# Gate and up products written to PSUM in unit order, with the stride moved into VectorE's transpose

## Chip, cores, metric

The kernel runs on one core of one Trainium2 chip. The metric is device time in microseconds (us) of one execution; a profile of one execution goes with each kernel. PE is TensorE, PEld the weight load that comes before each of its matmuls, DVE is VectorE, ACT is ScalarE. "Granted clock" is the share of full TensorE speed that the trace records.

## The reference, cut to what matters

One decode step of a transformer layer for one token: layer norm, attention over a cache of 4096 positions for 32 heads, a residual add, then layer norm and a gated MLP, which is where the change lies.

```python
# ... attention: q = norm(x) @ wq; softmax(q k^T) v for 32 heads x 4096 keys x 128; @ wo ...
g = jnp.einsum("bsd,df->bsf", x, w_gate)    # x: 1 x 640, w_gate: 640 x 1728
u = jnp.einsum("bsd,df->bsf", x, w_up)
h = _gelu(g) * u
return jnp.einsum("bsf,fd->bsd", h, w_down)  # w_down: 1728 x 640
```

All inputs are bf16. Four fifths of the 84.23 MB read are the K and V caches, each 32 x 4096 x 128 x 2 bytes = 33.6 MB.

## The kernel before

The MLP has one row of activations. Four row groups of the PE array (r = 0..3, output rows 0, 32, 64, 96) each compute 432 of the 1728 units, so that four matmuls run side by side; five such rounds (j, the chunks of 128 of the 640 inputs) accumulate. The 432 units of a row are 16 groups `i` of 27; each group serves two partitions `b`, 14 units `c` each (one unit is shared), hence 448 output columns. A transpose of 32x32 blocks on VectorE then turns each row into columns, so that unit values lie on partitions for the w_down product.

```python
DF = 1728; PER = 2; PAIR_UNITS = 27; NFC = 14; HP = 32; COLS = NFC * HP   # 448; values filled in here
WD = ((0, 8), (8, 11), (11, 13), (13, 14))     # w_down is loaded in four pieces of chunks

def up(ps, w, name):
    landed_once(name)                          # PE waits for the weights
    for j in range(DC):                        # 5
        for r in range(YR):                    # 4
            rhs = ...                          # [128, 16, 2 (step 13), 14]: runs of 14 bf16
            inst = PE.matmul(
                ps[32 * r : 32 * r + 1, :].rearrange("q (c i b) -> q i b c", c=NFC, b=PER),
                lhsT=hc[:, j : j + 1], rhs=rhs, start=False, stop=(j == DC - 1),
                skip_group_check=True, tile_position=(0, 32 * r))
    return inst

PE.wait_ge(S["dve"], D_HC)
end("g", up(g_ps, wg_sb, "wg"))
fill(6)                                        # fillers: matmuls nobody reads, meant to hold the PE clock up
end("u", up(u_ps, wu_sb, "wu"))
fill(2)
PE.wait_ge(S["dve"], D_HID)
for i, (a, b) in enumerate(WD):
    PE.wait_ge(S[f"wd{i}"], 16 * PER)          # y's matmuls wait for each piece of w_down
    for c in range(a, b):
        ...                                    # 4 matmuls of 160 columns each
end("y", inst)
# [cut] VectorE:
def turn_rows(col, ps):
    dve(lambda: DVE.transpose(col[:].rearrange("p c n -> p (c n)"), ps), False)

wait_pe(T["end", "g"]); turn_rows(g_col, g_ps)
# [cut] ten small operations of the GELU
wait_pe(T["end", "u"]); turn_rows(u_col, u_ps)
# [cut] hid_own, hid = gelu(g) * u;  then y_row = y_ps + h_row, and the store
# [cut] sync engine, in this order, one queue:
load("wg", ...); load("wu", ...)
SP.wait_ge(S["dve"], D_SCORES[NQ - SLOTS])
for i, (a, b) in enumerate(WD):
    for odd in range(PER):
        load(f"wd{i}", ...)                    # eight transfers, the last of the program's inputs
```

In the old order, consecutive outputs of a matmul (c, the innermost of its loop) lie 32 fp32, that is 128 bytes, apart in PSUM; the transpose reads its row contiguously.

The softmax here doesn't subtract the row's maximum and nothing guards it: scores larger than these inputs give would overflow.

Of the kernel before, what the change touches and what calls it, by code (L numbers as in the profile page):

```python
# [9 lines left out]
def kernel(  # L10
# [19 lines left out]
    PE, DVE, ACT, SP, POOL = nc.tensor, nc.vector, nc.scalar, nc.sync, nc.gpsimd  # L30
# [20 lines left out]
    PER = 2  # L51
    PAIR_UNITS = PER * DF // P
    NFC = (PAIR_UNITS + 1) // 2
# [102 lines left out]
    def tick(which, inst):  # L156
        inst.then_inc(S[which], 1)
        done[which] += 1
        return done[which]
# [6 lines left out]
    def wait(engine, which, value):  # L166
        if value > 0:
            engine.wait_ge(S[which], value)
# [8 lines left out]
    def landed_once(name):  # L177

        PE.wait_ge(S[name], 16)
        once.append(name)  # L180
# [4 lines left out]
    def dve(make, raw=True):  # L185

        if raw:
            wait(DVE, "dve", done["dve"])
        return tick("dve", make())
# [199 lines left out]
    def up(ps, w, name):  # L389


        landed_once(name)
        for j in range(DC):
            for r in range(YR):
                rhs = w[:, j, r * RG : (r + 1) * RG].rearrange("p (i f) -> p i f", f=PAIR_UNITS)
                rhs = bass.AP(
                    tensor=rhs.tensor,
                    offset=rhs.offset,
                    ap=[rhs.ap[0], rhs.ap[1], [PAIR_UNITS - NFC, PER], [1, NFC]],
                )  # L400
                inst = PE.matmul(
                    ps[32 * r : 32 * r + 1, :].rearrange("q (c i b) -> q i b c", c=NFC, b=PER),
                    lhsT=hc[:, j : j + 1],
                    rhs=rhs,
                    start=False,
                    stop=(j == DC - 1),
                    skip_group_check=True,
                    tile_position=(0, 32 * r),
# [5 lines that stand above are left out]
    fill(6)  # L414
# [3 lines that stand above are left out]
# [179 lines left out]
            turn_keys(m + 1, 1)  # L597

    def turn_rows(col, ps):
        dve(lambda: DVE.transpose(col[:].rearrange("p c n -> p (c n)"), ps), False)  # L600

    assert done["dve"] == D0
    wait_pe(pe_at(NQ - 1, "project"))
# [5 lines left out]
    assert var_of(hm, hv) == D_HV  # L609
    wait_pe(T["end", "g"])  # L610
    turn_rows(g_col, g_ps)
    DVE.wait_ge(S["r"], 2)
    dve(lambda: DVE.tensor_scalar(g_sb[:], g_col[:, :, 0], hr[:], None, op0=ALU.mult))
# [10 lines left out]
    dve(lambda: DVE.tensor_tensor(g_own[:], g_sb[:, ends], parity[:], op=ALU.mult))  # L624
    wait_pe(T["end", "u"])
    turn_rows(u_col, u_ps)
    dve(lambda: DVE.tensor_tensor(hid_own[:], g_own[:], u_col[:, ends, 0], op=ALU.mult))
    assert dve(lambda: DVE.tensor_tensor(hid[:], g_sb[:], u_col[:, :, 0], op=ALU.mult), False) == D_HID
# [50 lines left out]
```

## Time and profile before

| | before |
|---|---|
| time, median of three runs | 205.8 us (205.79 to 205.98) |
| bytes read from HBM | 84.23 MB, 413 GB/s over the span |
| busy: PE / DVE | 45% / 52% of the span |
| gate products (20 matmuls) | 190.27 to 194.17 us, clock 0.50 |
| up products (20 matmuls) | 195.78 to 197.83 us, clock 1.00 |
| the two row transposes | 0.65 us each |
| hid ready | 198.81 us |
| last y matmul ends | 200.91 us |

From the page of the kernel before: the span, two engines, and two rows that cut the span into 40 slices (tenths of DMA busy time, and GB/s moved).

```profile
span 203.9 us, 4088 instructions
...
PE 90.8 (45%) x1839; PEld 53.8 (26%) x1839; DVE 105.2 (52%) x185; ACT 4.5 (2%) x11; POOL 6.8 (3%) x12
...
DMA  7999999999999999999989999999899999999990
GB/s 249 410 466 411 418 456 437 437 411 416 450 434 386 463 450 424 418 424 444 444 381 467 450 418 418 431 437 456 383 424 437 431 418 437 431 418 433 421 375 23
```

The DMA engines are full from the second slice nearly to the end, so the kernel is as long as its bytes plus what comes before the first and after the last of them. PE and VectorE are each about half idle. A change to either matters only if its work lies after the last bytes, or holds up a transfer.

The chain of waits, the last pieces in order of time (start us, length us, what):

```profile
176.91 23.69 DMA big<-in_B_w_down_dram
...
200.64 0.27 PE y L378 x4
...
200.94 0.32 DVE y_row L630
```

One w_down transfer, queued at 176.91 us behind everything else, lands at 200.60, and only four y matmuls and an add follow it. Gate and up are not in the chain. The tail in the timeline (start us, length us, engine, line, what, [idle time before, and what ended it]):

```profile
190.27 3.90 PE L401 MATMUL g<-big,hc 128*1 128x448 bf16 x20
...
194.11 1.74 PE L369 MATMUL s<-ex,ident 128*128 128x512 bf16 x6
194.23 0.65 DVE L600 STREAM_TRANSPOSE g_col<-g 128x448 f32<-128x448 f32 x1 [3.44 <-PE g L401]
...
195.78 2.05 PE L401 MATMUL u<-big,hc 128*1 128x448 bf16 x20
...
197.88 0.65 DVE L600 STREAM_TRANSPOSE u_col<-u 128x448 f32<-128x448 f32 x1 [0.42 <-PE u L401]
...
198.64 0.17 DVE L628 TENSOR_TENSOR hid<-g_sb,u_col 128x14 bf16<-128x14 f32 x1
...
198.88 0.99 PE L378 MATMUL y<-big,hid 128*1 128x160 bf16 x42
...
200.28 0.60 PE L378 MATMUL y<-big,hid 128*1 128x160 bf16 x10 [0.41 <-DMA big<-in_B_w_down_dram]
200.64 0.08 PEld L378 LDWEIGHTS y<-big,hid 128*1 128x1 bf16 x2 [0.26 <-DMA big<-in_B_w_down_dram]
...
200.94 0.32 DVE L630 TENSOR_TENSOR y_row<-y,h_row 128x160 bf16<-128x160 f32 x1 [2.12 <-PE y L378]
```

Compute is ahead: 44 y matmuls run at once after hid, and then PE stands until 200.28 us for the third piece of w_down, and its weight loads until 200.64 us for the fourth and last. Five rounds of four gate matmuls took 3.9 us at half clock, and the same five rounds of up 2.05 us at full clock.

### The profile page before, as it was taken

The numbers are of one execution on the slowest core, as the hardware profiler recorded it, in microseconds if no ns is written. First come the engines' busy times: TensorE is split into PE (matmuls) and PEld (weight loads), VectorE is DVE, ScalarE is ACT, GpSimd is POOL, SyncE is SP. The second block draws the span as 40 slices with busy tenths as digits, with TensorE's granted clock in tenths as the row PEclk, the third lists the DMA queues.
The fourth block names the chain that finished last, engine by engine and source line by source line (L and its number), as shares of the span: only waits on it lengthen the run. The fifth ranks groups of instructions, "written<-read, shape, count | busy, mean of one in ns | idle before, by whom it ended". The sixth has DMA issues, their size and how long they took to land. (4 is left out here: it accounts for less than half of the span.)

```text
span 203.9 us, 4088 instructions
## 1 busy us (share of the span) xinstructions
PE 90.8 (45%) x1839; PEld 53.8 (26%) x1839; DVE 105.2 (52%) x185; ACT 4.5 (2%) x11; POOL 6.8 (3%) x12
## 2 busy tenths in 40 slices
PE   0003603516642862066307640484166358258993
PEld 0001100115312711062107310451063154046221
DVE  5003399480649467509570957064908582632260
ACT  2000100000000000000000000000000000000000
POOL 8301000000000000000000000000000000000100
PEclk9999965555555555556755555555555755555597
DMA  7999999999999999999989999999899999999990
GB/s 249 410 466 411 418 456 437 437 411 416 450 434 386 463 450 424 418 424 444 444 381 467 450 418 418 431 437 456 383 424 437 431 418 437 431 418 433 421 375 23
DMA packets 4405, 84.30 MB, mean 413 GB/s; under 512 B 560, under 2 KB 688, under 8 KB 944
## 3 DMA queue, kind: packets, MB, share of 16 engines
q1 hardware_dynamic: 4400, 84.23, 96.8%
q8 instruction: 3, 0.05, 0.1%
q14 instruction: 2, 0.02, 0.0%
HBM read 84.23 MB, written 0.00 MB: 413 GB/s over the span
## 5 line engine op out<-in xcount | busy, mean ns | idle before, releaser
L561 DVE STREAM_TRANSPOSE big<-big 128x1024 f32<-128x1024 f32 x64 | 73.7, 1210 | 6.4 <-issue 4.0
L273 PE MATMUL o<-ex,big 128*128 128x4 bf16 x1024 | 28.6, 166 | 37.0 <-PEq L173 37.0
L245 PE MATMUL s<-big,q_quad 128*8 128x512 bf16 x256 | 28.7, 594 | 23.8 <-DVE big L561 23.8
L273 PEld LDWEIGHTS o<-ex,big 128*128 128x128 bf16 x1024 | 28.4, 104 | 37.4 <-issue 37.4
L588 DVE TENSOR_TENSOR o_col<-o,rinv 128x4 bf16<-128x4 f32 x8 | 1.3, 162 | 37.2 <-PE o L273 37.2
L245 PEld LDWEIGHTS s<-big,q_quad 128*8 128x8 bf16 x256 | 7.0, 112 | 40.7 <-DVE big L561 32.1
L570 DVE STREAM_TRANSPOSE s_turned<-s 128x512 f32<-128x512 f32 x8 | 5.7, 717 | 14.3 <-PE s L245 14.3
L280 PE MATMUL a<-wo,o_row 128*1 128x160 bf16 x256 | 9.9, 333 | 2.3 <-DVE o_row L595 2.3
L292 PE MATMUL t<-rs_cur,ones_f 128*128 128x4 f32 x16 | 4.7, 366 | 10.1 <-DVE rs_cur L581 10.1
L573 DVE TENSOR_TENSOR ex<-e,of_head 128x512 bf16<-128x512 f32 x8 | 5.5, 691 | 6.8 <-PE e L261 6.8
L302 PE MATMUL o<-x_col,mean_f 128*128 128x10 f32 x2 | 0.6, 376 | 16.7 <-DVE x_col L210 16.7
L280 PEld LDWEIGHTS a<-wo,o_row 128*1 128x1 bf16 x256 | 7.1, 115 | 3.0 <-DVE o_row L595 3.0
L261 PE MATMUL e<-e_part,ident 128*32 128x32 bf16 x128 | 2.5, 196 | 10.1 <-PEq L340 10.1
L292 PEld LDWEIGHTS t<-rs_cur,ones_f 128*128 128x128 f32 x16 | 4.0, 313 | 11.1 <-DVE rs_cur L581 11.1
L445 POOL TENSOR_TENSOR hr<-hv,half_f 128x1 f32<-128x1 f32 x1 | 0.6, 553 | 172.1 <-DVE hv L219 172.1
L223 DVE CAST x_row<-x_69 128x160 f32<-128x160 bf16 x1 | 0.2, 243 | 11.5 <-DMA x_69<-in_A_x_dram 11.5
L261 PEld LDWEIGHTS e<-e_part,ident 128*32 128x32 bf16 x128 | 1.8, 106 | 16.4 <-issue 16.4
L513 ACT ACTIVATE e_part<-s_turned 128x128 bf16<-128x128 f32 x8 | 2.5, 308 | 153.2 <-DVE s_turned L570 153.2
L302 PEld LDWEIGHTS o<-x_col,mean_f 128*128 128x128 f32 x2 | 0.5, 313 | 16.7 <-DVE x_col L210 16.7
L295 PE MATMUL o<-col_of,o_spread 128*128 128x8 bf16 x8 | 1.5, 188 | 7.0 <-issue 3.5
L441 POOL MEMSET wo<- 128x5120 bf16 x1 | 4.4, 4368 | 0.0
L318 PE MATMUL g<-big,xn_bf 128*1 128x512 bf16 x20 | 3.2, 623 | 1.9 <-DVE xn_bf L230 1.9
(84 smaller groups left out, 48.1 us busy)
## 6 DMA issues: line engine op xcount, KB each, us to landing
big<-in_A_k_cache_dram SPq DMA_DIRECT2D x7, 4096.0 KB, 20.2
big<-in_A_v_cache_dram SPq DMA_DIRECT2D x6, 4096.0 KB, 17.7
big<-in_A_v_cache_dram SPq DMA_DIRECT2D x4, 2048.0 KB, 12.3
big<-in_A_wq_dram SPq DMA_DIRECT2D x1, 5120.0 KB, 15.2
wo<-in_A_wo_dram SPq DMA_DIRECT2D x4, 1280.0 KB, 15.6
big<-in_A_k_cache_dram SPq DMA_DIRECT2D x2, 2048.0 KB, 17.2
big<-in_B_w_gate_dram SPq DMA_DIRECT2D x1, 2160.0 KB, 18.5
big<-in_B_w_up_dram SPq DMA_DIRECT2D x1, 2160.0 KB, 23.2
```

What stands on the lines that cost most here:

```text
L245: inst = PE.matmul(s_bank[32 * r : 32 * r + 2 * QH, :], lhsT=q_quad[:, 2 * k + e, (1 - b) * QH : (3 - b) * QH], rhs=kt_at[:, k, HALF * b + ...
L261: inst = PE.matmul(to[32 * h : 32 * h + 32, r], lhsT=ident[:, 32 * r : 32 * r + 32], rhs=e_part[:, :, :, h], start=True, stop=True, tile_p ...
L273: inst = PE.matmul(o_ps, lhsT=vt[:, j, :], rhs=e_t[:, j, :], start=(j == 0), stop=(j == NB - 1))
L280: inst = PE.matmul(attn_ps[32 * r : 32 * r + 1, :], lhsT=o_row[:, j : j + 1], rhs=wo_t[:, j, r * YW : (r + 1) * YW], start=False, stop=j = ...
L292: mark("totals", PE.matmul(ps, lhsT=ones_f[:], rhs=rs_cur[:], start=True, stop=True))
L295: inst = PE.matmul(ps, lhsT=o_spread[:].rearrange("p h c -> p (h c)"), rhs=col_of[:], start=True, stop=True)
L318: inst = PE.matmul(qr_ps[b][32 * r : 32 * r + 1, :], lhsT=xn_bf[:, c : c + 1], rhs=wq_sb[:, c, :].rearrange("p (m h d) -> p m h d", h=QH, ...
L441: POOL.memset(t[:], 0.0).then_inc(S["pool"], 1)
L513: ACT.activation(e_part[:].rearrange("p b j h -> p j b h"), s_turned[:, :, 0 : 2 * QH].rearrange("p j (b h) -> p j b h", b=2), AF.Exp, sca ...
L561: DVE.transpose(to[:, c], of[:, c].rearrange("p (j k n) -> p j k n", k=2, n=HP)).then_inc(S["kt"], 1)
L570: assert dve(lambda: DVE.transpose(s_turned[:].rearrange("p j n -> p (j n)"), s_bank[:]), False) == D_SCORES[m]
L573: DVE.tensor_tensor(e_t[:], e_ps.unsqueeze(2).broadcast_to(shape), of_head[:].unsqueeze(1).broadcast_to(shape), op=ALU.mult,).then_inc(S[" ...
```

## The change

The output is written in the order i, b, c, so that a matmul writes 448 consecutive fp32; VectorE's transpose picks up every 14th fp32 instead. Nothing else differs, and the order of instructions on every engine is the same. The intent is to speed up the products.

```diff
@@ up() @@
-                    ps[32 * r : 32 * r + 1, :].rearrange("q (c i b) -> q i b c", c=NFC, b=PER),
+                    ps[32 * r : 32 * r + 1, :].rearrange("q (i b c) -> q i b c", c=NFC, b=PER),
@@ turn_rows() @@
-        dve(lambda: DVE.transpose(col[:].rearrange("p c n -> p (c n)"), ps), False)
+        dve(lambda: DVE.transpose(col[:], ps.rearrange("q (p c) -> q c p", c=NFC)), False)
```

## The prediction

> **What bounds the kernel now.** The memory queue. The page's slices show the 16 DMA engines 90% or more busy in nearly every slice of the 203.9 us span (84.23 MB at 413 GB/s); PE is busy 45%, VectorE 52%. The chain of waits ends in one 23.69 us piece, the last w_down transfer (176.91 to 200.60 us), then 0.27 us of y matmuls, 0.32 us of the last add, and the store.
>
> **The stage that changes.** From the timeline of the tail: 20 gate matmuls 190.27 to 194.17 us at granted clock 0.50; six fillers to 195.85; 20 up matmuls 195.78 to 197.83 at clock 1.00; the two row transposes 0.65 us each; hid ready at 198.81; 44 y matmuls 198.87 to 199.86; then PE waits twice for w_down (until 200.28 and 200.64). Without those waits y would end near 200.15, not 200.91 (estimate: 199.86 plus twelve matmuls at the same pace). So compute is already about 0.8 us ahead of the last bytes.
>
> **What the change does.** No instruction is added, removed or moved on any engine. Two access patterns change.
> 1. Gate and up matmuls write 448 consecutive fp32 of PSUM instead of 128-byte steps. Now four concurrent row groups of 448 columns take 0.74 us at clock 0.50 and 0.38 us at 1.00, about twice per column what the query matmuls pay (512 columns, contiguous, about 0.445 us a group at 0.5). The Trainium skill, "PSUM — Partial Sum Buffer", Specifications, says any non-contiguous pattern slows matmuls significantly; this trace agrees, by a factor of about 2. I expect gate near 2.0 us (3.9 before) and up near 1.0 us (2.05).
> 2. The two transposes read PSUM in 56-byte steps. The trace's contiguous ones (448 elements 649 ns, 512 elements 717 ns) extrapolate to about 343 ns for 160; the strided 160-element one takes 461 ns. Scaled to 448 this estimates 0.98 us each, +0.33; range 0.8 to 1.3.
>
> Gate values come about 1.6 us earlier, but up waits for the fillers and its weights (issued about 172.0, 23.2 us to landing, so about 195.2); it starts about 0.5 us earlier, ends about 1.5 us earlier, and hid comes about 1.2 us earlier (near 197.6).
>
> **How much is critical.** None. The last w_down bytes still land near 200.6; the gain becomes a longer PE wait for w_down. No DMA issue depends on these instructions: the queue's last wait for compute before the store (near 171 us) lies before the changed stage.
>
> **Second order.** PE idles more from 197 to 200 us, so its clock could fall to 0.5 before the last y matmuls: at most +0.1 to 0.2 us.
>
> **Prediction:** 205.8 us, range 205.3 to 206.2; faster by over 2%: 0.01, within 2%: 0.98, slower: 0.01.
>
> **What would show it right.** Gate matmuls spanning about 2.0 us, up about 1.0; the g and u transposes near 980 ns; hid about a microsecond earlier; y's waits on w_down longer in sum; the chain still ending in w_down near 200.6 us; total within 0.3 us.
>
> **What would make it wrong.** If the doubled matmul time comes from the moving operand (runs of 14 elements), not the output, gate and up stay slow, and the dearer transposes delay hid by 0.3 to 0.7 us: still inside the slack, still about 205.8. If a strided transpose cost over 1.5 us, hid would pass the last bytes and the time would rise by tenths. If the last bytes land earlier than read here, a gain could show, at most about 0.7 us, well under 2%.

## The result, and the profile after

| | before | after |
|---|---|---|
| time, median of four runs each | 205.86 us (205.79 to 205.98) | 205.90 us (205.80 to 206.03) |
| gate products, from first start to last end | 3.90 us | 2.04 us |
| up products | 2.05 us | 1.18 us |
| one row transpose | 649 ns | 650 ns |
| hid ready | 198.81 us | 197.80 us |
| end of PE's last wait for w_down | 200.64 us | 200.94 us |

The ratio is 1.0002, 95% interval 0.9985 to 1.0019: no change is seen, and one of more than 0.2% is excluded. A ratio here is always the mean time of one kernel's fast runs over that of the other kernel's fast runs of the same rounds, so it is not quite the ratio of the medians quoted. Results are correct. The two profiles are of single executions at the two ends of the spread: the one before took 205.66 us, less than any of the timed runs above, and the one after 206.03 us, the slowest of its four.

The same rows of the page, after:

```profile
span 204.2 us, 4088 instructions
...
PE 89.1 (44%) x1839; PEld 53.7 (26%) x1839; DVE 105.2 (52%) x185; ACT 4.5 (2%) x11; POOL 6.8 (3%) x12
...
DMA  7999999999999999999999999999999999999980
GB/s 249 401 474 411 411 456 456 424 411 416 443 452 391 456 443 417 411 449 443 436 386 481 424 411 424 456 443 424 394 428 433 430 420 433 430 423 432 416 359 19
```

The same bytes at the same pace; PE lost 1.7 us of busy time. The chain of waits, last pieces:

```profile
175.68 24.86 DMA big<-in_B_w_down_dram
200.58 0.70 PE y L378 x12
201.30 0.33 DVE y_row L630
```

It still runs through a w_down transfer. The one that it names lands at 175.68 + 24.86 = 200.54 us, but it is the third piece, and the chain before named the fourth. The chain view misses the wait for the fourth here, since by the modelled ends some of the matmuls from 200.58 us were still running when it landed. The timeline shows it: the weight loads of the last four matmuls waited until 200.94 us. The tail:

```profile
190.31 2.04 PE L401 MATMUL g<-big,hc 128*1 128x448 bf16 x20
...
192.28 1.99 PE L369 MATMUL s<-ex,ident 128*128 128x512 bf16 x6
192.40 0.65 DVE L600 STREAM_TRANSPOSE g_col<-g 128x448 f32<-128x448 f32 x1 [1.57 <-PE g L401]
...
195.63 1.18 PE L401 MATMUL u<-big,hc 128*1 128x448 bf16 x20 [1.36 <-DMA big<-in_B_w_up_dram]
...
196.87 0.65 DVE L600 STREAM_TRANSPOSE u_col<-u 128x448 f32<-128x448 f32 x1 [1.23 <-PE u L401]
...
197.63 0.17 DVE L628 TENSOR_TENSOR hid<-g_sb,u_col 128x14 bf16<-128x14 f32 x1
...
198.78 0.23 PE L378 MATMUL y<-big,hid_own 128*1 128x160 bf16 x2 [1.43 <-DMA big<-in_B_w_down_dram]
...
198.78 0.72 PE L378 MATMUL y<-big,hid 128*1 128x160 bf16 x30
...
199.82 0.38 PE L378 MATMUL y<-big,hid 128*1 128x160 bf16 x12 [0.32 <-DMA big<-in_B_w_down_dram]
...
200.58 0.66 PE L378 MATMUL y<-big,hid 128*1 128x160 bf16 x10 [0.38 <-DMA big<-in_B_w_down_dram]
200.94 0.08 PEld L378 LDWEIGHTS y<-big,hid 128*1 128x1 bf16 x2 [0.26 <-DMA big<-in_B_w_down_dram]
...
201.30 0.33 DVE L630 TENSOR_TENSOR y_row<-y,h_row 128x160 bf16<-128x160 f32 x1 [3.49 <-PE y L378]
```

Compare line by line. The gate products are 1.86 us shorter. Up starts only 0.15 us earlier, since it now waits 1.36 us for its weights; it is 0.87 us shorter, and hid comes 1.01 us earlier. Then PE waits for all four pieces of w_down (until 198.78, 199.82, 200.58 and 200.94 us). The saved microsecond has become waiting time there.

The last add starts at 201.30 us instead of 200.94, 0.36 us later. Of this 0.30 us is the landing: PE's last wait ended at 200.94 us and not at 200.64. The landing records say the same (200.90 against 200.60 us; they are semaphore updates kept in the packed trace, of which `prof` prints only the waits that they end). They also show a spread: with w_down in eight transfers the last piece landed at 200.60, 200.76 and 200.89 us in three traces of the kernel before and its variants, and at 200.73 to 201.05 us in six of the changed kernel and its variants. The two ranges overlap; whether the change has any part in the shift is not shown, and the times of the two kernels do not differ. The other 0.06 us goes with the granted clock, which the windows view shows (columns: stretch, its length, busy time of each engine with the number of instructions, PE clock, DMA share, GB/s):

```profile
199.80:200.90 1.10, 0.62 (x18) 0.19 (x12) 0.00 (x0) 0.00 (x0) 0.00 (x0) 1.00 0.09 27
```

```profile
200.50:201.30 0.80, 0.67 (x12) 0.19 (x12) 0.00 (x1) 0.00 (x0) 0.00 (x0) 0.50 0.00 0
```

In this run of the changed kernel the clock had fallen to 0.50 for the last y matmuls. The 0.70 us of the last twelve in the chain is not the price of that, since it holds the wait until 200.94 us. Experiment 4 comes back to it.

### The profile page after: what moved, and what is told of

Its sections match the earlier page's. It is cut to its first block, busy times and chain, and to the rows that moved or that the text cites. A ratio compares the mean times of both kernels' runs of the same rounds, so it can differ in the third digit from the quotient of the medians.

```text
span 204.2 us, 4088 instructions
## 1 busy us (share of the span) xinstructions
PE 89.1 (44%) x1839; PEld 53.7 (26%) x1839; DVE 105.2 (52%) x185; ACT 4.5 (2%) x11; POOL 6.8 (3%) x12
## 5 line engine op out<-in xcount | busy, mean ns | idle before, releaser
L245 PE MATMUL s<-big,q_quad 128*8 128x512 bf16 x256 | 29.6, 609 | 24.1 <-DVE big L561 24.1
L223 DVE CAST x_row<-x_69 128x160 f32<-128x160 bf16 x1 | 0.2, 244 | 11.4 <-DMA x_69<-in_A_x_dram 11.4
L369 PE MATMUL s<-ex,ident 128*128 128x512 bf16 x11 | 4.2, 499 | 0.0
## 6 DMA issues: line engine op xcount, KB each, us to landing
big<-in_B_w_up_dram SPq DMA_DIRECT2D x1, 2160.0 KB, 23.5
```

The lines of the kernel that those rows point to most:

```text
L245: inst = PE.matmul(s_bank[32 * r : 32 * r + 2 * QH, :], lhsT=q_quad[:, 2 * k + e, (1 - b) * QH : (3 - b) * QH], rhs=kt_at[:, k, HALF * b + ...
L369: PE.matmul(s_bank[:], lhsT=ident[:], rhs=e_t[:].rearrange("p j h -> p (j h)"), start=True, stop=True)
```

## The experiments

My theory: the change does what was meant in its stage, about 1.0 us, and the w_down transfer covers all of it. Its rivals: the stage does not really get shorter to its end (up waits for its weights, so nothing but idle time is won); or the end is set by something else than w_down; or something gained is given back elsewhere (transposes, clock).

### 1. Take the w_down transfers away, from both kernels

```diff
-    SP.wait_ge(S["dve"], D_SCORES[NQ - SLOTS])
-            load(f"wd{i}", ...)
+            pass
-        PE.wait_ge(S[f"wd{i}"], 16 * PER)
-        POOL.sem_inc(S[f"wd{i}"], -16 * PER)
```

The y products then read old K data: the result is wrong.

> The kernel before without its w_down transfers (y then reads old K data: wrong on purpose). My theory: w_down's landing is what ends both kernels, and compute stands only 0.8 us behind it here, so the time falls by 0.6 to 1.0 us, to about 205.0 us, and the chain of waits ends in y, hid and the up transpose instead of a w_down transfer. Rival (the end is set by compute, or by something fixed): no change, or the fall is that of 2.2 MB at 413 GB/s, about 5 us.

> The changed kernel without its w_down transfers (wrong on purpose). My theory: with the transfer gone the saving of the change becomes visible: hid was ready 1.0 us earlier (197.80 against 198.81), so this is 0.8 to 1.4 us faster than before_nowd, about 204.0 us. Rival (the change saves nothing of the tail because up waits for its weights, whatever the matmuls take): within 0.3 us of before_nowd.

Measured in the same rounds: kernel before 205.97 us; before without w_down 204.67 us (ratio 0.9947, 0.9932 to 0.9961); after without w_down 203.66 us (ratio 0.9890, 0.9875 to 0.9905). The two differ by 1.01 us (medians of five and of four runs; 0.85 us between the two profiled runs), as the theory said, and the intervals do not overlap. The timeline of each without w_down:

```profile
195.49 2.05 PE L401 MATMUL u<-big,hc 128*1 128x448 bf16 x20
...
198.59 1.13 PE L378 MATMUL y<-big,hid 128*1 128x160 bf16 x52
```

```profile
195.42 1.26 PE L401 MATMUL u<-big,hc 128*1 128x448 bf16 x20 [0.29 <-DMA big<-in_B_w_up_dram]
...
197.73 1.13 PE L378 MATMUL y<-big,hid 128*1 128x160 bf16 x52
```

No y matmul waits any more, and y starts right after hid. The fall of 1.30 us of the kernel before is more than the 0.6 to 1.0 us that I expected. Part of this is that I reckoned from the profile before, whose run was 0.31 us faster than the median here (205.66 against 205.97 us). Part is seen in the profile: up started at 195.49 us there and not at 195.78, as the six fillers ahead of it took 1.47 us and not 1.74 (the clock had risen earlier). y ended at 199.75 us instead of 200.91, 1.16 us sooner; less those 0.29 us, the slack in front of w_down is 0.87 us. The rival of 5 us (the bytes themselves) is out, because the tail's compute, not the transfer, then ends the kernel.

### 2. Make the tail's compute longer by the same amount, in both kernels

```diff
     end("u", up(u_ps, wu_sb, "wu"))
-    fill(2)
+    fill(18)
```

> The kernel before with 16 more filler matmuls (about 3.45 us at full clock) between the up matmuls and y, w_down loaded as usual. My theory: the fillers eat the 0.8 us of slack and the rest shows: y starts near 201.65, ends near 202.95 instead of 200.91: +1.7 to +2.3 us, about 207.9 us. Rival (slack is larger than I read): less than +1 us.

> The changed kernel with the same 16 fillers. My theory: up ends 1.0 us earlier, so y starts near 200.65 and ends near 201.95: +0.6 to +1.2 us, about 206.9 us, which is 0.8 to 1.2 us less than before_fill. Rival (the change has no effect on when hid or up end): same as before_fill within 0.3 us.

Measured: before with the fillers 207.47 us (ratio 1.0087, 1.0073 to 1.0101), after with the fillers 206.52 us (ratio 1.0030, 1.0016 to 1.0043), against 205.97 us for the kernel before. The timeline of y in each, in that order:

```profile
201.49 1.12 PE L378 MATMUL y<-big,hid 128*1 128x160 bf16 x52
```

```profile
200.75 1.13 PE L378 MATMUL y<-big,hid 128*1 128x160 bf16 x52
```

Both rises (1.50 and 0.55 us) are a little under what I expected, because I had again reckoned from the fast run of the profile before: between single profiles they are 1.74 us (207.40 - 205.66) and 1.01 us (206.67 - 205.66), inside both expectations. The difference of the medians, 0.95 us, is what the theory gives; between the two profiled runs it is 0.73 us, as up waited for its weights until 195.64 us in the second and started at 195.51 us in the first. With w_down loaded as always, the microsecond appears in the time once compute is the later of the two. So the change does shorten the stage to its end, and the rival that only idle time is won falls.

### 3. What a step costs, measured by itself

Into the idle start of the changed kernel, before x and wq arrive, went eight transposes on VectorE and, after 16 warming matmuls, six sets of twelve matmuls (three rounds of the four row groups, 448 columns each). The operand is the matrix that streams through the array (`rhs`); an "even" one is read without gaps, the kernel's own comes in runs of 14.

```diff
+    dve(lambda: DVE.transpose(flat, src))                                      # SBUF, 448, contiguous
+    dve(lambda: DVE.transpose(g_col[:], src.rearrange("q (p c) -> q c p", c=14)))  # SBUF, step 14
+    ...                                        # the same for 160 (step 5), and all four from PSUM (g_ps)
+    PE.matmul(...)  # L355 even operand, contiguous output
+    PE.matmul(...)  # L358 operand in runs of 14, contiguous output    (the changed kernel)
+    PE.matmul(...)  # L361 operand in runs of 14, output "q (c i b)"   (the kernel before)
+    PE.matmul(...)  # L364 even operand, output steps of 128 bytes
+    PE.matmul(...)  # L367 even operand, output steps of 8 bytes
+    PE.matmul(...)  # L370 even operand, pairs of neighbours in steps of 128 bytes
```

> The changed kernel with probes in the idle time at its start. VectorE transposes of 448 and 160 fp32 per partition, from SBUF and from PSUM, contiguous and in steps (14 for 448, 5 for 160). Theory A (a step costs in SBUF, not in PSUM): SBUF 160 contiguous near 350 ns and in steps 461; SBUF 448 contiguous near 650 and in steps near 950 or more; all PSUM ones equal to their contiguous form. Theory B (no step costs anything; the 160 one just has a larger fixed part): SBUF and PSUM, contiguous and stepped, equal in pairs, the 160 ones all near 460. TensorE, after 16 warming matmuls, three rounds of four row groups of 448 columns each: contiguous output, even or 14-element-run operand: near 0.19 us a round at full clock; the old output order with the run operand, and 128-byte steps with an even operand: near 0.38 us if the output is what costs (theory C); if the operand's runs cost (theory D), the run operand with contiguous output is slow and the 128-byte steps with an even operand fast. 8-byte steps: theory C says slow too if what counts is two neighbours per step, fast if only large steps cost; pairs of neighbours in 128-byte steps: fast under the first, slow under the second.

One run (206.04 us, correct, state unknown; nothing is read from its time). By source line (durations in ns, shortest/median/longest; L223 to L230 are in the order SBUF 448 plain, step 14, SBUF 160 plain, step 5, then the same four from PSUM):

```profile
L223 DVE STREAM_TRANSPOSE g_col<-u_col x1: 647/647/647, 4.8 to 4.8; 128x448 f32<-128x448 f32 x1
...
L224 DVE STREAM_TRANSPOSE g_col<-u_col x1: 952/952/952, 5.5 to 5.5; 128x448 f32<-128x448 f32 x1
...
L225 DVE STREAM_TRANSPOSE g_col<-u_col x1: 345/345/345, 6.5 to 6.5; 128x160 f32<-128x160 f32 x1
...
L226 DVE STREAM_TRANSPOSE g_col<-u_col x1: 479/479/479, 6.9 to 6.9; 128x160 f32<-128x160 f32 x1
...
L227 DVE STREAM_TRANSPOSE g_col<-g x1: 650/650/650, 7.4 to 7.4; 128x448 f32<-128x448 f32 x1
...
L228 DVE STREAM_TRANSPOSE g_col<-g x1: 651/651/651, 8.1 to 8.1; 128x448 f32<-128x448 f32 x1
...
L229 DVE STREAM_TRANSPOSE g_col<-g x1: 349/349/349, 8.8 to 8.8; 128x160 f32<-128x160 f32 x1
...
L230 DVE STREAM_TRANSPOSE g_col<-g x1: 350/350/350, 9.1 to 9.1; 128x160 f32<-128x160 f32 x1
...
L355 PE MATMUL y<-ex,ident x12: 350/351/352, 6.8 to 7.2; 128*1 128x448 bf16 x12
...
L358 PE MATMUL y<-ex,ident x12: 366/366/366, 7.3 to 7.8; 128*1 128x448 bf16 x12
...
L361 PE MATMUL y<-ex,ident x12: 539/575/575, 8.0 to 8.7; 128*1 128x448 bf16 x12
...
L364 PE MATMUL y<-ex,ident x12: 575/581/581, 9.0 to 9.8; 128*1 128x448 bf16 x12
...
L367 PE MATMUL y<-ex,ident x12: 581/581/581, 10.2 to 10.9; 128*1 128x448 bf16 x12
...
L370 PE MATMUL y<-ex,ident x12: 352/353/394, 11.3 to 11.7; 128*1 128x448 bf16 x12
```

On VectorE theory A holds: a single-element step costs when the source is SBUF (952 against 647 ns for 448, 479 against 345 for 160) and nothing when it is PSUM (651 against 650, 350 against 349). My prediction had taken the price of a step from the transpose of h_row, which reads SBUF, and applied it to a PSUM read. The Trainium skill, "Vector Engine (DVE) Microarchitecture Reference", section 5.2 (Measured stream behaviour on trn2, the passage on the SBUF access granule), puts a hop at every element at about 0.65 cycle, and more for small steps. In this run a step costs (952 - 647) / 448 = 0.68 ns an element at step 14 and (479 - 345) / 160 = 0.84 ns at step 5. A contiguous element takes (647 - 345) / 288 = 1.05 ns; if that is a cycle (an estimate), step 14 costs 0.65 cycle and step 5 0.80, which agrees in size and in direction. The passage speaks of SBUF only, and I should have read it so.

On TensorE theory C holds: the output order alone makes the difference. With the same operand, the old order (575 ns) is slower than the new (366 ns), and an even operand does not rescue a stepped output (581 ns). The operand's runs of 14 cost 15 ns at most (366 against 351). (366 and 575 ns are also the medians of the up matmuls after and before, which ran at clock 1.00.) From start to start, a set with contiguous output took 0.57 to 0.60 us and one with stepped output 1.10 to 1.12 us for its three rounds, so 0.19 to 0.20 and 0.37 us a round. In the two steps tried, what counts is neighbours, not distance: 8-byte steps are as slow as 128-byte steps, and pairs of neighbours 128 bytes apart are as fast as contiguous output (353 against 351 ns). That is the rule of the Trainium skill, "Advanced Engine Details and Errata", Memory Cachelines, PSUM Cachelines, that every two consecutive elements should be contiguous.

### 4. Two attempts to use the slack

First, w_down in four transfers rather than eight.

```diff
-    WD = ((0, 8), (8, 11), (11, 13), (13, 14))
+    WD = ((0, 11), (11, 14))
```

> An attempt at a faster version: w_down in four transfers rather than eight (11 and 3 chunks instead of 8, 3, 2, 1), since in the changed kernel y only waits for w_down. Theory: the last bytes land at the same time and the y matmuls left after them grow from 4 to 12 (+0.2 us), so 205.8 to 206.2 us, no gain. Rival (small transfers delay the end of the queue): the last landing moves forward by 0.5 us or more and the time falls to 205.5 us or less.

Measured 205.89 us (205.68 to 206.96) against 205.97 us, ratio 1.0006, 0.9988 to 1.0023: no gain. The first piece now let y start only at 199.75 us, and the last add began at 201.16. The last landing did not move forward by half a microsecond: 200.68 us in the landing records, against 200.73 and 200.90 us in the two traces of the unaltered changed kernel.

Second, the clock. The fall to 0.50 near the end suggested eight fillers after up instead of two, still ending before w_down's first pieces land; the opposite, no fillers at all, shows what they are worth.

```diff
     end("u", up(u_ps, wu_sb, "wu"))
-    fill(2)
+    fill(8)            # after_fill8;  after_nofill removes this and the fillers fill(2), fill(1), fill(6) ahead of it
```

> The changed kernel unaltered, on the same chip and in the same rounds as the two that follow. Theory: within 0.2 us of the kernel before.

> The changed kernel with 8 fillers after up instead of 2 (1.7 us, ending near 198.5, before the first w_down chunks land near 198.75). The profile of the changed kernel shows its granted clock falling to 0.50 near 200 us, so that the last twelve y matmuls took 0.70 us. Theory (that fall costs something): with a fuller window the clock stays at 1.00 to the end and the time falls by 0.1 to 0.25 us, to about 205.75. Rival (the last matmuls wait for the landing anyway): no difference beyond 0.1 us. Either way no more than 0.3 us is to be had.

> The changed kernel with all fillers of the tail removed (11 matmuls). Theory: up and y run at clock 0.50; up's end and hid come 0.9 us later, which the wait for w_down absorbs, and only the last y matmuls show: +0.1 to +0.3 us. Rival (the slack is smaller than I think, or y at half clock falls behind the landings): +0.5 us or more. Second rival (the clock doesn't matter at all): 0.0.

| kernel, five runs each, same rounds | median (range), us | ratio to before | interval |
|---|---|---|---|
| before | 205.92 (205.79 to 206.07), 9 runs | | |
| after_again | 206.11 (205.88 to 206.27) | 1.0008 | 0.9995 to 1.0022 |
| after_fill8 | 205.93 (205.86 to 206.08) | 0.9999 | 0.9985 to 1.0012 |
| after_nofill | 205.98 (205.85 to 206.31) | 1.0000 | 0.9987 to 1.0014 |

Every interval holds 1 and they overlap, so no difference is shown. after_fill8 lies 0.18 us below after_again, the size that I expected, but the times are inconclusive: in the profiled run of after_again the clock stayed at 1.00 to the end of y without any extra fillers, so the fall is not in every run. In the clock records the full clock lasted 6.8 us in both traces of the unaltered changed kernel, from 193.4 us in the one and from 195.9 us in the other, and 10.2 us with eight fillers, from 193.9 us.

The traces give the price of the fall. From the end of PE's last wait to the start of the last add there are 0.30 us in the kernel before (200.64 to 200.94), 0.29 in after_again (200.77 to 201.06) and 0.30 in after_fill8 (200.97 to 201.27), all at clock 1.00, and 0.36 us in the changed kernel's first profile (200.94 to 201.30) and in after_nofill (201.09 to 201.45), both at 0.50. So the fall costs 0.06 us, less than the 0.1 to 0.25 us that I expected, and less than the landing moves from run to run.

That the changed kernel needs no fillers was expected as +0.1 to +0.3 us and came out as nothing measurable. In its profile up and y ran at clock 0.50, up took 2.04 us, and w_down still ended the last waits.

Then the kernel before without its fillers:

> The kernel before with all 11 fillers of the tail removed, to set beside after_nofill (no change in time). Theory: up waits for its weights near 195.6, takes 3.8 us at clock 0.50 as the gate matmuls do, hid comes near 200.5, y takes 1.6 us at half clock and ends near 202.2 instead of 200.9: +0.9 to +1.6 us, about 207.2 us. Rival (the clock rises without the fillers, or the wait for w_down still absorbs it): within 0.3 us of the kernel before.

Measured 206.00 us (205.77 to 206.73) against 206.00 us, ratio 0.9996, 0.9982 to 1.0010. My expectation of +0.9 to +1.6 us missed. The profiled run is the slowest of the five, 206.73 us, and it shows what I had described, only smaller:

```profile
195.62 3.80 PE L399 MATMUL u<-big,hc 128*1 128x448 bf16 x20 [1.35 <-DMA big<-in_B_w_up_dram]
...
200.47 1.13 PE L376 MATMUL y<-big,hid 128*1 128x160 bf16 x52
```

Up took 3.80 us, and y started at 200.47 us and had no wait for w_down any more. But the clock rose during up's last rounds, so y took 1.13 us and not 1.6. The other four runs (205.77 to 206.03 us) did not pay; their traces are not kept, so that the clock rose earlier in them is a guess. I had argued from one phase of the clock as if every run had it.

## Why the prediction was right

- **The bound (right).** w_down's last piece ends both kernels: PE waited for it until 200.64 us before and 200.94 after. I had foreseen the landing near 200.6 us again; the 0.3 us between the two is within the spread of the landing from run to run. Experiment 1 shows it from the other side: without that transfer the changed kernel is 2.31 us shorter than the kernel before with it (205.97 - 203.66).
- **Products (right, with one term short).** Gate: about 2.0 us foreseen, 2.04 measured. Up: about 1.0 foreseen, 1.18 measured. I had counted five rounds and left out the time from the last start to its end, which the old 2.05 us contains too. That the output and not the operand was the cause is shown by the probe. One support of the estimate was weak: the trace has no clock record before 24.0 us, so the 0.5 that I gave for the query matmuls was inferred. The score matmuls, also 512 columns, keep the same pace at a recorded 0.50 (starts of the groups 0.42 us apart).
- **Transposes (wrong).** The step "scaled to 448 this estimates 0.98 us each, +0.33" failed: 650 ns, +0.00. The price was taken from a transpose that reads SBUF; from PSUM a step is free (651 against 650 ns).
- **When hid comes (right in kind, two errors that cancelled).** Foreseen 197.6 us, measured 197.80. Up started at 195.63 us and not near 195.3, since its weights, like the later pieces of w_down, landed about 0.3 us later in this run than in the profile before (172.08 + 23.5 against 172.04 + 23.2 us); the transposes, dearer in the sum than on the chip, made up for it. The gain at hid was 1.01 us instead of 1.2.
- **What is critical: none (right).** Slack in front of w_down was put at 0.8 us and came out at 0.87 us by the profiles of experiment 1. That is the slack in a run whose w_down landed early; where it lands later there should be more, which was not measured. The saved time is real (1.01 us without w_down, 0.95 us with extra fillers; 0.85 and 0.73 us between single profiles) and is spent waiting for w_down.
- **Second order (right in kind, too large).** The clock did fall to 0.50 before the last matmuls in the profiled run, but not in every run. Up to 0.1 to 0.2 us were allowed for it; the traces show 0.06 us between the last wait and the last add, which the spread of the times hides.

## What to carry to other kernels

Before counting what a faster stage is worth, find what its result waits beside: here a transfer that lands later than the result is needed covers a saving that is real and repeatable. To show where such a saving went, remove the covering transfer, or lengthen the stage equally in both kernels, and see whether the difference returns. Look at more than one profile before reading a cause into tenths of a microsecond: here the last landing alone moved between 200.60 and 201.05 us. When a layout needs a stride somewhere, let TensorE write at least pairs of neighbours and put the single-element stride into VectorE's read of PSUM, found to be free (transposes of 32x32 blocks, steps of 5 and 14 fp32).

## What the Trainium skill lacked or had wrong

- "PSUM — Partial Sum Buffer", Specifications, says that any non-contiguous pattern slows matmuls significantly, and "Advanced Engine Details and Errata", PSUM Cachelines, repeats it. Too broad: pairs of neighbouring fp32 in 128-byte steps took 353 ns a matmul against 351 ns contiguous, while single elements in 8-byte or 128-byte steps took 575 to 581 ns. The other sentence of PSUM Cachelines, that every two consecutive elements should be contiguous, is the one that fits.
- Neither page gives a size. Here: 0.37 us a round of four row groups of 448 columns against 0.19 us at clock 1.00, and 0.74 us before against 0.37 us after the change at clock 0.50, so about a factor of 2 at either clock.
- "Vector Engine (DVE) Microarchitecture Reference", section 5.2, gives the price of single-element steps for SBUF and not for PSUM. Here a transpose reading PSUM pays nothing: 448 elements in steps of 14 took 651 ns against 650 ns contiguous, and from SBUF 952 against 647 ns.
